# A TensorE planner that waits for room for two projections: half-array work, attention banks and the first loads of an attention and FFN kernel

## The chip, the cores and the metric

The kernel runs on one core of a Trainium2 chip. Times are device microseconds (us) of one execution. The kernel before takes 367.8 us (median of 3, 367.53 to 368.38). Most executions of one kernel agree within some 0.3%. A profile adds nothing visible: the profiled execution of before took 367.36 us by the same clock, of which 365.6 us lie between its first and last instruction ("span").

## The reference, cut to what matters

```python
# B=8 batches, H=8 heads, S=576 positions, D=64, 128 features; then an FFN over 4608 tokens
def phi(x):                                  # x: q or k
    proj = einsum('bhsd,df->bhsf', x, w_phi)
    proj = proj - max(abs(proj), axis=-1)
    return concatenate([exp(proj), exp(-proj)], axis=-1)
q_p, k_p = phi(q), phi(k)
kv  = einsum('bhsf,bhsd->bhfd', k_p, v);  z = sum(k_p, axis=2)
num = einsum('bhsf,bhfd->bhsd', q_p, kv)
den = einsum('bhsf,bhf->bhs', q_p, z)[..., None] + 1e-6
x   = (num / den) rearranged to [4608, 512]
out = square(relu(x @ w_in)) @ w_out         # w_in [512, 2048], w_out [2048, 512]
```

The heads have 64 channels, so the projections and the kv product use 64 of TensorE's 128 rows ("half-array" work, two row halves side by side). The product of q features with kv and the whole FFN use 128 rows ("full-array" work). By the ledger below, the FFN is 249 of 316 us of useful TensorE time.

## The kernel before

The kernel does not issue instructions in the order of its source. Every piece of work becomes an operation with a cost, a key (its place in a list of FFN units), its dependencies and its buffers. A planner then runs a small model of the engines and the loads, and the order that it finds is the program. In the trace of before, all 4,069 recorded matmuls of TensorE start in exactly this order, so a wrong guess of the planner becomes a wait on the chip. The part that chooses TensorE's next operation:

```python
SWITCH = 96
AHEAD, GROUP, LATE = 12, 2, 4

def pick(self, q, rows, can):
    now = min((it[0] for it in q if it[2].rows == 128), default=None)
    half = sorted(it for it in q if it[2].rows == 64 and can(it[2]))
    if now is None or now < 1 or not half:
        return None
    if rows == 64:                       # already in half-array work: stay
        go = half[0][0] < now + self.AHEAD
    else:                                # start it when one is late or two are overdue
        go = half[0][0] < now - self.LATE or (
            len([it for it in half if it[0] < now]) >= self.GROUP)
    # ... go: the first of half; otherwise the first full-array operation that can run
```

`can` asks whether the operation's buffers are free. All PSUM tiles come from one ring of eight banks; an attention operation takes a second token beside its bank, so that attention never holds more than `NATT` banks:

```python
NATT, LEAD, DUE, SPAN = 6, 3, 34, 28
r_one = ring("one", 8, [P, 512], F32, ps)      # eight PSUM banks
r_att = Ring(list(range(NATT)))                # tokens for attention
def banks(n):
    w = [Buf(r_one) for _ in range(n)]
    for x in w:
        x.token = Buf(r_att)
    return w
```

The first loads, all issued from GpSimd's queue, and what depends on them:

```python
FIRSTS = "k0 v0 q0 win k1 v1 wout q1"    # k0, v0, q0 in two halves, the rest whole
# ... ffn_in waits for all of w_in, ffn_out for all of w_out:
p_ = pe(key, 4 * (2 + TCH * 0.418), fn, xT_ops[c][a:z] + [o_win], [w, xT])
p_ = pe(key, 865, fn, [h2[c, mc, tt][2] for mc in mcs] + [o_wout], [w, out_] + ...)
```

In batches 0 and 1 ("fold") the maximum is not subtracted from k's projection; exp is taken from PSUM directly, and v is scaled by exp of the maximum instead, on GpSimd (line 523; in batch 1 five of the ten scalings run on VectorE). In the other batches VectorE subtracts the maximum (line 487, tile `ksh`), and v is only copied:

```python
if not fold:
    nc.vector.tensor_tensor(out=ksh.t[...], in0=wv(e), in1=mk.t[...], op=ALU.subtract)   # frees the PSUM bank
    # exp(+-) from ksh on ScalarE
else:
    # exp(+-) from PSUM on ScalarE, then for each of five groups and both signs:
    nc.gpsimd.tensor_tensor(out=y.t[...], in0=xv.t[...], in1=y.t[..., D]..., op=ALU.mult)
```

While TensorE has nothing to do in the start, the planner lets it multiply ones ("fillers"). Most operations of batch 0 come before the first FFN matmul; those of batches 1 to 7 are mixed with FFN work.

Of the kernel before, what the change touches and what calls it, by code (L numbers as in the profile page):

```python
# [45 lines left out]
class Plan:  # L46
# [30 lines left out]
    AHEAD, GROUP, LATE = 12, 2, 4  # L77

    def pick(self, q, rows, can):
# [4 lines left out]
        if rows == 64:  # L84
            go = half[0][0] < now + self.AHEAD
        else:
            go = half[0][0] < now - self.LATE or (
                len([it for it in half if it[0] < now]) >= self.GROUP)
# [97 lines left out]
def kernel(  # L186
# [10 lines left out]
    nc = tc.nc  # L197
# [51 lines left out]
    FOLD, VON = 2, ((1, 1), (0, 1))  # L249
    KTD = 1  # L250
    N0 = 43, 51
    NATT, LEAD, DUE, SPAN = 6, 3, 34, 28
# [6 lines left out]
    MARGIN = 200  # L259
    att = []  # L260

    def pe(key, cost, fn, deps=(), bufs=(), rows=128):
        o = pl.op("pe", cost, key, fn, deps, bufs, lat=350, rows=rows)
        att.append(o)
        return o

    def act(key, n, fn, deps=(), bufs=()):
        return pl.op("act", 60 + 0.83 * n, key, fn, deps, bufs, lat=220 + MARGIN)

    def dve(key, n, fn, deps=(), bufs=()):  # L270

        return pl.op("dve", 65 + 1.04 * n, key, fn, deps, bufs, lat=190 + MARGIN)

    def pool(key, cost, fn, deps=(), bufs=()):
        return pl.op("pool", cost, key, fn, deps, bufs, lat=150 + MARGIN)
# [56 lines left out]
    def load_x(b, name, key, dep=None, parts=1):  # L332

        t, r = src[name]
        buf = Buf(r)
        rows = t[b].rearrange("h s d -> (h s d)").rearrange("(pr t c) -> t pr c", pr=NPR, t=P)

        def fn(a, z):
# [4 lines left out]
        n = NPR // parts  # L343
        got[b, name] = buf, [[load(key + i / 10, 295 * n, 128 * n,
                                   lambda a=i * n: fn(a, a + n), [dep], [buf])]
                             for i in range(parts)]
# [4 lines left out]
    FIRSTS = "k0 v0 q0 win k1 v1 wout q1"  # L351
    for n, what in enumerate(FIRSTS.split()):
        if what == "win":
            o_win = load(FIRST + n, 4194, 512, lambda: nc.gpsimd.dma_start(out=win, in_=win_v))
        elif what == "wout":
            o_wout = load(FIRST + n, 4194, 2048,
                          lambda: nc.gpsimd.dma_start(out=wout, in_=wout_v))
        else:
            load_x(int(what[1]), what[0], FIRST + n, None, 2 if what[1] == "0" else 1)
# [29 lines left out]
    def attention(b, key):  # L389
# [5 lines left out]
        def transposes(xb, ld, xt, at):  # L395

            ops = []
            if b >= NPE[at]:
                for u0, n in GRP:
# [5 lines left out]
                    ops.append(xbar(key(at), n * 16, fn, ld[0] + (lq[0] if b > 1 else []), [xb, xt]))  # L405
                return ops
            for u0, n in ((0, 16), (16, 16), (32, 4)) if b or at else GRP:
                w, = banks(1)

                def fn(u0=u0, n=n, w=w):  # L410
                    for i in range(n // 2):
# [5 lines left out]
                        [o_id] + ld[0] + (ld[-1] if u0 + n > U // 2 else []), [w, xb, xt])  # L417
# [15 lines left out]

        tk = transposes(xk, lk, kT, 0)
# [8 lines left out]
        fold = b < FOLD  # L443
        va = [Buf(r_va), Buf(r_va)] if fold else [Buf(r_va)] * 2
        o_va = [[], []]
        if not fold:
            def fn():
                nc.gpsimd.memset(va[0].t[:, :, D], 1.0)
                nc.gpsimd.tensor_copy(out=va[0].t[:, :, :D], in_=xv.t)
            o_va = [[pool(key(32), 2400, fn, lv[0] + lv[-1], va[:1] + [xv])] * NG] * 2  # L450
# [4 lines left out]
        for g, (u0, n) in enumerate(GRP):  # L455
# [26 lines left out]
            if not fold:  # L482
# [10 lines left out]
                for t, sg in zip(ph, (1.0, -1.0)):  # L493
# [5 lines left out]
                    ke.append(act(kk, 2 * c, fn, d1, [t, ksh]))  # L499
# [13 lines left out]
            for s_, (y, sg) in enumerate(zip(va, (-1.0, 1.0))):  # L513
# [12 lines left out]
                deps = [o] + lv[0] + (lv[-1] if u0 + n > U // 2 else [])  # L526
# [12 lines left out]
        for hf in range(2):  # L539
# [6 lines left out]
            for prl in range(2):  # L546
                pr = 2 * hf + prl
                for s in range(2):
                    def fn(w=w, pr=pr, prl=prl, s=s):
                        for j in range(NJ):  # L550
# [3 lines left out]
                            for hi in range(2):  # L554
# [4 lines left out]
                                    rhs=va[s].t[r, u, : D + 1],  # L559
                                    start=(j == 0), stop=(j == NJ - 1))  # L560
                    gs = {(NJ * pr + j) // 8 for j in range(NJ)}
                    ops.append(pe(key(KV_AT[b > 0] + 8 * hf + 2 * (2 * prl + s)), 285, fn,
                                  [o_va[s][g] for g in gs] + [o for g in gs for o in (ke[2 * g + s] if fold else [ke[2 * g + s]])],
                                  w + [va[s]] + [kph[g][s] for g in gs], 64))
# [16 lines left out]
        for i, (g0, j0, nj) in enumerate(order_j):  # L581
# [144 lines left out]
            if hi_ == P and b == 0:  # L726
# [164 lines left out]
```

## Time and profile before

| | before |
|---|---|
| time, median | 367.8 us |
| span | 365.6 us |
| TensorE busy | 353.7 us (97%) |
| first FFN input matmul | 28.1 us |
| first FFN output matmul | 44.8 us |
| half-array runs on TensorE | 93 |

The page of the kernel before, cut: engines with busy time, share and instructions; then busy tenths in 40 slices of 9.1 us; then the chain of work that ended last.

```profile
span 365.6 us, 10343 instructions
...
PE 353.7 (97%) x4069; PEld 200.0 (55%) x4069; DVE 246.5 (67%) x553; ACT 242.3 (66%) x501; POOL 186.0 (51%) x289
...
PE   8899799999999999999999999999999999999994
...
POOL 8855745458837881787538764785445600000000
PEclk9999899999999999999999999999999999999999
DMA  7999962559755975488656944595520331121133
...
PE 82%; DVE 6%; DMA 3%; POOL 3%; SPq 2%; issue 2%; ACT 1%; DVEq 0%; POOLq 0%; ACTq 0%
```

TensorE is nearly always busy and owns 82% of the chain. The load engines are full from the second to the fifth slice (tenths of 9). But busy time is modelled from overlapping matmuls and hides what the engine loses, so the starts of matmuls have to be read. The timeline of TensorE alone (start us, duration us, engine, line, operation, output and inputs, rows x columns of the weights, size):

```profile
243.67 0.81 PE L762 MATMUL one<-xT,win 128*128 128x512 bf16 x3
244.31 0.29 PE L700 MATMUL one<-kv_sb,qph 128*128 128x65 bf16 x4
244.53 0.40 PE L632 MATMUL one<-wphi,qT 64*128 64x128 bf16 x8
244.86 0.39 PE L791 MATMUL one<-wout,h 128*128 128x512 bf16 x1
```

Read from start to start: four 65-column matmuls take 0.22 us here instead of the 4 x 31 ns that they take in a row, then eight half-array matmuls take 0.33 us before the next full-array one. Over the trace, from 60 us on, the medians are exact to some ns: a 512-column matmul is followed after 216 ns by another full-array matmul, and after 312 ns by a half-array one (48 cases). A 65-column matmul is followed after 31 ns by another, but after 125 to 128 ns by a half-array one. Back from half to full array the same 93 to 96 ns are lost. So each change of the array costs about 95 ns, and each half-array run two of them, 0.19 us.

That allows a ledger. *Useful* is each matmul at its steady start-to-start time as read from the trace (216 ns for 512 columns, 109 for 256, 56 for 128, 31 for 65; half-array pairs of 256 and 128 columns about 109 and 56; kv 16 each). *Changes* are array changes times 95 ns. *Fillers* are the ones-matmuls. *Gaps* are the rest between the first and the last matmul. Up to 47 matmul records of the output half are missing in some traces; they are counted as useful at 216 ns. A group of like matmuls that straddles 50 us is booked whole before it, so the useful work of a "0 to 50" column can be up to 0.9 us too high; cut strictly at 50 us it is 24.1 us before.

| ledger of before, us | 0 to 50 | from 50 | all |
|---|---|---|---|
| useful | 25.0 | 291.5 | 316.5 |
| changes | 3.4 | 14.2 | 17.7 (186) |
| fillers | 11.0 | 0 | 11.0 |
| gaps | 10.3 | 4.0 | 14.4 |

With 1.2 us before the first matmul and 4.8 us after the last one this adds up to the span. Useful work can't go away, so a gain must come from the start (25 us of use in 50 us), from changes or from gaps.

The waits of TensorE from 50 to 345 us name 1.8 of the 4.0 us of later gaps (engine, line, releaser: us, times, longest):

```profile
PE one L762 <- DVE ksh L487: 0.7, 1, 0.7
PE one L632 <- DMA qT<-xq: 0.6, 1, 0.6
PE one L600 <- DVE ksh L487: 0.3, 1, 0.3
PE one L791 <- DVE m L653: 0.2, 1, 0.2
```

In the start, GpSimd scales v. Its timeline from 9 to 24 us:

```profile
10.67 1.05 POOL L523 TENSOR_TENSOR va<-xv,va 128x512 bf16<-128x512 bf16 x1 [2.15 <-DMA xv<-in_v_dram]
11.68 1.22 POOL L357 DMA_DIRECT2D wout<-in_moe_w_out_dram  x1
12.91 3.09 POOL L523 TENSOR_TENSOR va<-xv,va 128x512 bf16<-128x512 bf16 x3
...
16.77 5.25 POOL L523 TENSOR_TENSOR va<-xv,va 128x512 bf16<-128x512 bf16 x6
```

The scalings end at 22.0 us, with w_out's issue among them; the first FFN matmul follows 6 us later. And in the page's fifth slice the granted clock falls (length, then busy us and count of each engine, granted clock, DMA share, GB/s):

```profile
core 0: us, PE busy (x) PEld busy (x) DVE busy (x) ACT busy (x) POOL busy (x), PEclk, DMA share, GB/s
40.00:43.40 3.40, 1.83 (x36) 1.55 (x33) 3.40 (x7) 3.40 (x10) 3.11 (x3) 1.00 1.22 209
43.40:46.80 3.40, 3.39 (x31) 1.68 (x28) 3.40 (x12) 2.49 (x7) 2.88 (x4) 0.50 1.21 207
```

For 3.4 us TensorE has half its clock (0.50), after 3.4 us in which it was busy for 1.83 us only.

### The profile page before, as it was taken

The page shows a single profiled execution, that of the slowest core. Times are in us where ns is not written, and L with a number is a line of the kernel's source. Part 1 is how long each engine was busy: PE and PEld are TensorE (multiplying, and loading weights), DVE is VectorE, ACT ScalarE, POOL GpSimd, SP SyncE. Part 2 cuts the span into 40 slices and gives each one's busy share as a digit, 9 for nine tenths or more (in the row PEclk, how much of TensorE's full clock was granted, in tenths as well). Part 3 has the DMA queues.
Part 4 walks back from the last instruction along what each step waited for, and adds up shares of the span by engine and source line. Part 5 has one row for each costly group of instructions (what it writes and reads, how often), then busy time and mean ns, then how long its engine had stood idle before and what let it go on. Part 6 is the DMA issues. An engine that isn't in the chain of part 4 may idle for free.

```text
span 365.6 us, 10343 instructions
## 1 busy us (share of the span) xinstructions
PE 353.7 (97%) x4069; PEld 200.0 (55%) x4069; DVE 246.5 (67%) x553; ACT 242.3 (66%) x501; POOL 186.0 (51%) x289
## 2 busy tenths in 40 slices
PE   8899799999999999999999999999999999999994
PEld 6679576766654555455545554454445544444442
DVE  2779969894789589868596868875886743332321
ACT  2997979689739983997479846985699633333300
POOL 8855745458837881787538764785445600000000
PEclk9999899999999999999999999999999999999999
DMA  7999962559755975488656944595520331121133
GB/s 110 208 209 208 208 119 59 90 85 166 133 102 81 173 147 103 87 161 157 94 102 113 176 96 100 90 216 87 109 64 22 74 82 34 29 48 41 29 72 73
DMA packets 68257, 39.81 MB, mean 109 GB/s; under 512 B 48624, under 2 KB 63088, under 8 KB 68208
## 3 DMA queue, kind: packets, MB, share of 16 engines
q0 software_dynamic: 15312, 18.35, 30.3%
q1 hardware_dynamic: 52896, 20.79, 28.7%
q8 instruction: 32, 0.52, 0.6%
q14 instruction: 17, 0.14, 0.1%
HBM read 36.77 MB, written 9.44 MB: 126 GB/s over the span
## 4 chain that ended last, share of the span: by engine, by line
PE 82%; DVE 6%; DMA 3%; POOL 3%; SPq 2%; issue 2%; ACT 1%; DVEq 0%; POOLq 0%; ACTq 0%
PE one L791 32%; PE one L762 31%; PE one L700 6%; PE one L556 4%; PE one L600 3%; PE one L632 3%; DVE mk L477 2%; POOL va L523 2%; DMA xv<-in_v_dram 2%; DVE ksh L487 2%; PE one L466 2%; SPq L401 2%; DMA qT<-xq 1%; PE one L366 1%; DVE ot L798 1%
## 5 line engine op out<-in xcount | busy, mean ns | idle before, releaser
L770 POOL TENSOR_TENSOR h<-hr 128x512 bf16<-128x512 bf16 x112 | 115.8, 1042 | 87.1 <-ACT hr L767 85.0
L762 PE MATMUL one<-xT,win 128*128 128x512 bf16 (+2 forms) x768 | 145.7, 326 | 0.9 <-DVE ksh L487 0.7
L791 PE MATMUL one<-wout,h 128*128 128x512 bf16 x576 | 145.9, 381 | 0.2 <-DVE m L653 0.2
L767 ACT ACTIVATE hr<-one 128x512 bf16<-128x512 f32 x144 | 85.3, 606 | 77.8 <-PE one L762 69.6
L762 PEld LDWEIGHTS <-win 128*128 128x128 bf16 x768 | 66.0, 98 | 50.4 <-issue 1.8
L791 PEld LDWEIGHTS <-h 128*128 128x128 bf16 x576 | 51.8, 98 | 57.3 <-issue 2.6
L607 ACT ACTIVATE qph<-one 128x512 bf16<-128x512 f32 (+1 forms) x160 | 78.0, 572 | 7.0 <-PE one L600 5.8
L495 ACT ACTIVATE kph<-ksh 128x1024 bf16<-128x1024 f32 (+1 forms) x60 | 54.9, 969 | 11.4 <-DVE ksh L487 10.9
L477 DVE TENSOR_REDUCE mk<-one 128x4 f32<-128x512 f32 (+1 forms) x80 | 49.3, 625 | 5.5 <-PE one L466 5.5
L653 DVE TENSOR_REDUCE m<-one 128x4 f32<-128x512 f32 (+1 forms) x60 | 35.5, 628 | 18.6 <-PE one L632 12.8
L798 DVE COPY ot<-one 128x512 f32<-128x512 f32 x36 | 24.7, 686 | 27.1 <-PE one L791 26.8
L710 DVE TENSOR_TENSOR one<-one,em 128x260 f32<-128x260 f32 (+1 forms) x80 | 32.0, 430 | 13.2 <-PE one L700 11.0
L487 DVE TENSOR_TENSOR ksh<-one,mk 128x512 f32<-128x512 f32 (+1 forms) x60 | 38.3, 638 | 3.3
L700 PEld LDWEIGHTS <-qph 128*128 128x128 bf16 x640 | 30.1, 98 | 16.4 <-issue 3.2
L700 PE MATMUL one<-kv_sb,qph 128*128 128x65 bf16 x640 | 34.7, 194 | 1.3 <-ACT kph L508 1.3
L721 DVE TENSOR_TENSOR xo<-one,rden 128x256 bf16<-128x256 f32 (+1 forms) x80 | 31.3, 417 | 0.6
L773 DVE TENSOR_TENSOR h<-hr 128x512 bf16<-128x512 bf16 x32 | 13.5, 422 | 23.3 <-ACT hr L767 23.3
L662 POOL COPY mq<-m 64x4 f32<-64x4 f32 x108 | 20.0, 185 | 9.4 <-DVE m L653 5.6
L556 PE MATMUL one<-va,kph 64*128 64x65 bf16 x1152 | 23.9, 191 | 0.2
L556 PEld LDWEIGHTS <-kph 64*128 64x128 bf16 x1152 | 21.2, 94 | 4.9 <-issue 4.4
L508 ACT ACTIVATE kph<-one 128x512 bf16<-128x512 f32 (+1 forms) x40 | 19.6, 605 | 2.1 <-DVE mk L477 2.1
L366 PE MATMUL one<-ones 128*128 128x256 bf16 x101 | 16.4, 305 | 1.2 <-DVE scrap L312 1.2
(46 smaller groups left out, 209.1 us busy)
## 6 DMA issues: line engine op xcount, KB each, us to landing
out_dram<-ot SPq DMA_DIRECT2D x72, 128.0 KB, 2.4
xk<-in_k_dram POOLq DMA_DIRECT2D x7, 576.0 KB, 6.4
xv<-in_v_dram POOLq DMA_DIRECT2D x7, 576.0 KB, 9.0
xq<-in_q_dram POOLq DMA_DIRECT2D x7, 576.0 KB, 11.8
win<-in_moe_w_in_dram POOLq DMA_DIRECT2D x1, 2048.0 KB, 18.8
wout<-in_moe_w_out_dram POOLq DMA_DIRECT2D x1, 2048.0 KB, 29.8
xk<-in_k_dram POOLq DMA_DIRECT2D x2, 288.0 KB, 5.3
xv<-in_v_dram POOLq DMA_DIRECT2D x2, 288.0 KB, 7.5
```

What stands on the lines that cost most here:

```text
L477: nc.vector.tensor_reduce(out=mk.t[:, e, ms], in_=wv(e), axis=AX.X, op=ALU.max, apply_absolute_value=True)
L487: nc.vector.tensor_tensor(out=ksh.t[:, e, : n // 2, :], in0=wv(e), in1=mk.t[:, e, ms].to_broadcast([P, n // 2, Fd]), op=ALU.subtract)
L495: nc.scalar.activation(out=t.t[:, :, : n // 2, :].rearrange("x e i f -> x e (i f)"), in_=ksh.t[:, :, : n // 2, :].rearrange("x e i f -> x ...
L556: nc.tensor.matmul(out=kvp(w, hi)[:, 2 * prl + s], lhsT=kph[g][s].t[r, i % 2, i // 2, :], rhs=va[s].t[r, u, : D + 1], start=(j == 0), stop ...
L607: nc.scalar.activation(out=t.t.rearrange("f (r b) hi p -> f b r hi p", b=2)[:, bk, :, :, lo:hi_], in_=w[bk].t[:, : nj * 256].rearrange("f ...
L653: d1 = [dve(kk, nj * 256, lambda w=w, m0=m0, nj=nj, bk=bk: nc.vector.tensor_reduce(out=m0.t[:, bk, : 2 * nj], in_=w[bk].t[:, : nj * 256].r ...
L700: nc.tensor.matmul(out=w.t[:, z * P : z * P + D + 1], lhsT=qg[s].t[:, h // 2, h % 2, :], rhs=kv[r][0].t[:, z % 2, z // 2, s, :], start=(s ...
L710: nc.vector.tensor_tensor(out=x, in0=x, in1=em.t[lo:hi_, hs].to_broadcast(list(x.shape)), op=ALU.mult)
L762: nc.tensor.matmul(out=w.t[:, y * n : (y + 1) * n], lhsT=win[:, kc, mc * P : (mc + 1) * P], rhs=xT.t[:, a:z, kc, :], start=(kc == 0), stop ...
L767: o = act(key - 4, TCH, lambda: nc.scalar.activation(out=r.t, in_=w.t, func=ACT.Relu), [p_], [w, r])
L770: o = pool(key - 4, 1050, lambda: nc.gpsimd.tensor_tensor(out=t.t, in0=r.t, in1=r.t, op=ALU.mult), [o], [r, t])
L791: nc.tensor.matmul(out=w.t, lhsT=h2[c, mc, tt][0].t[:, h2[c, mc, tt][1] :][:, :P], rhs=wout[:, mc, :], start=(mc == 0), stop=(mc == KC2 - 1))
```

## The change

Its intent, in its own words: TensorE's planner issues half-array work only when two projections fit into the free PSUM banks together, or when one is late; attention may hold seven banks; k0 is loaded in parts. The diff holds more than that: both weight matrices come in halves, each FFN group waits only for its half, and batches 0 and 1 scale v for three of the five groups; for the other two they subtract on VectorE like the later batches. The five scalings of batch 1 that VectorE made are moved or dropped with that. The planner's safety margins are cut in batch 0, batch 0's kv matmuls wait for fewer groups (`KVJ`), and the loads after the ninth get a later place in the plan.

```diff
-    AHEAD, GROUP, LATE = 12, 2, 4
+    AHEAD, GROUP, LATE = 24, 400, 8
+    EARLY = 3, 8
@@ pick, when TensorE is in full-array work
-            go = half[0][0] < now - self.LATE or (
-                len([it for it in half if it[0] < now]) >= self.GROUP)
+            go = half[0][0] < now - self.LATE
+            if not go and half[0][0] < now + self.EARLY[0]:
+                free, work = {}, 0
+                for it in half:
+                    if it[0] > now + self.EARLY[1]:
+                        break
+                    # ... need: how many buffers of each ring this operation still has to take
+                    if all(free.get(r, len(r.free)) >= n for r, n in need.items()):
+                        for r, n in need.items():
+                            free[r] = free.get(r, len(r.free)) - n
+                        work += it[2].cost
+                go = work >= self.GROUP
@@
-    FOLD, VON = 2, ((1, 1), (0, 1))
+    KVJ = 1
+    FG, VON = (3, 3), ((1, 1), (1, 1))       # groups of batches 0 and 1 that scale v
-    NATT, LEAD, DUE, SPAN = 6, 3, 34, 28
+    NATT, LEAD, DUE, SPAN = 7, 3, 34, 28
@@ margins of the planner
-    MARGIN = 200
+    MARGIN = 200
+    M0 = 40, 200, 350
+    slack = [M0[0]]                          # ... used for batch 0 in place of MARGIN
@@ first loads
-    FIRSTS = "k0 v0 q0 win k1 v1 wout q1"
+    FIRSTS = "k0:0-1 k0:1-2 k0:2-4 v0:0-2 v0:2-4 q0:0-2 q0:2-4 win:0-8 win:8-16 k1:0-4 v1:0-4 wout:0-8 q1:0-4 wout:8-16"
@@ ffn_in, ffn_out
-    ... xT_ops[c][a:z] + [o_win], [w, xT])
+    ... xT_ops[c][a:z] + [o_win[i * per + y] for y in range(per)], [w, xT])
-    ... for mc in mcs] + [o_wout],
+    ... for mc in mcs] + [o_wout[mc] for mc in mcs],
```

More of the change, by code (lines that the diff above doesn't have):

```diff
@@ L86, in pick @@
         else:
-            go = half[0][0] < now - self.LATE or (
-                len([it for it in half if it[0] < now]) >= self.GROUP)
+            go = half[0][0] < now - self.LATE
[4 more added lines that the diff above has]
+                        break
+                    new = {x for x in it[2].bufs if x.slot is None}
+                    need = {}
+                    for x in new:
+                        need[x.ring] = need.get(x.ring, 0) + 1
+                    if all(free.get(r, len(r.free)) >= n for r, n in need.items()):
[3 more added lines that the diff above has]
+                go = work >= self.GROUP
         if go:
@@ L247 @@
     r_ot = ring("ot", 2, [P, DM], F32)
-    FOLD, VON = 2, ((1, 1), (0, 1))
+    KVJ = 1
+    FG, VON = (3, 3), ((1, 1), (1, 1))
     KTD = 1
     N0 = 43, 51
-    NATT, LEAD, DUE, SPAN = 6, 3, 34, 28
+    PAIRS, XPE = 1, 1
+    NATT, LEAD, DUE, SPAN = 7, 3, 34, 28
     r_one = ring("one", 8, [P, 512], F32, ps)
@@ L259 @@
     MARGIN = 200
+    M0 = 40, 200, 350
+    slack = [M0[0]]
     att = []
     def pe(key, cost, fn, deps=(), bufs=(), rows=128):
-        o = pl.op("pe", cost, key, fn, deps, bufs, lat=350, rows=rows)
+        o = pl.op("pe", cost, key, fn, deps, bufs, lat=350 if slack[0] >= 100 else 240, rows=rows)
         att.append(o)
@@ L267, in act @@
     def act(key, n, fn, deps=(), bufs=()):
-        return pl.op("act", 60 + 0.83 * n, key, fn, deps, bufs, lat=220 + MARGIN)
+        return pl.op("act", 60 + 0.83 * n, key, fn, deps, bufs, lat=220 - 70 * (slack[0] < 100) + slack[0])
     def dve(key, n, fn, deps=(), bufs=()):
-        return pl.op("dve", 65 + 1.04 * n, key, fn, deps, bufs, lat=190 + MARGIN)
+        return pl.op("dve", 65 + 1.04 * n, key, fn, deps, bufs, lat=190 - 60 * (slack[0] < 100) + slack[0])
     def pool(key, cost, fn, deps=(), bufs=()):
-        return pl.op("pool", cost, key, fn, deps, bufs, lat=150 + MARGIN)
+        return pl.op("pool", cost, key, fn, deps, bufs, lat=150 + slack[0])
     queue, issues = [], []
@@ L330, with load_x, fn @@
     got = {}
-    def load_x(b, name, key, dep=None, parts=1):
+    def load_x(b, name, key, dep=None, a=0, z=NPR):
         t, r = src[name]
-        buf = Buf(r)
+        if (b, name) not in got:
+            got[b, name] = Buf(r), []
+        buf, parts = got[b, name]
         rows = t[b].rearrange("h s d -> (h s d)").rearrange("(pr t c) -> t pr c", pr=NPR, t=P)
-        def fn(a, z):
+        def fn():
             nc.gpsimd.dma_start(
@@ L342, in fn @@
             )
-        n = NPR // parts
-        got[b, name] = buf, [[load(key + i / 10, 295 * n, 128 * n,
-                                   lambda a=i * n: fn(a, a + n), [dep], [buf])]
-                             for i in range(parts)]
+        parts.append((a * NJ, load(key, 295 * (z - a), 128 * (z - a), fn, [dep], [buf])))
     win_v = moe_w_in.rearrange("(kc p) m -> p kc m", p=P)
@@ L350 @@
     o_id = pool(FIRST + 0.05, 700, lambda: make_identity(nc, ident))
-    FIRSTS = "k0 v0 q0 win k1 v1 wout q1"
+    FIRSTS = "k0:0-1 k0:1-2 k0:2-4 v0:0-2 v0:2-4 q0:0-2 q0:2-4 win:0-8 win:8-16 k1:0-4 v1:0-4 wout:0-8 q1:0-4 wout:8-16"
+    NEXT = 9
+    o_win, o_wout = {}, {}
     for n, what in enumerate(FIRSTS.split()):
+        what, a = what.split(":")
+        a, z = (int(x) for x in a.split("-"))
+        at = FIRST + n if n < NEXT else -160 + n
         if what == "win":
-            o_win = load(FIRST + n, 4194, 512, lambda: nc.gpsimd.dma_start(out=win, in_=win_v))
+            x = slice(a * P, z * P)
+            o = load(at, 262 * (z - a), 512, lambda x=x: nc.gpsimd.dma_start(
+                out=win[:, :, x], in_=win_v[:, :, x]))
+            o_win.update({mc: o for mc in range(a, z)})
         elif what == "wout":
-            o_wout = load(FIRST + n, 4194, 2048,
-                          lambda: nc.gpsimd.dma_start(out=wout, in_=wout_v))
+            o = load(at, 262 * (z - a), 128 * (z - a),
+                     lambda a=a, z=z: nc.gpsimd.dma_start(out=wout[:, a:z], in_=wout_v[:, a:z]))
+            o_wout.update({mc: o for mc in range(a, z)})
         else:
-            load_x(int(what[1]), what[0], FIRST + n, None, 2 if what[1] == "0" else 1)
+            load_x(int(what[1]), what[0], at, None, a, z)
     def loads(b, dep):
@@ L404, in fn @@
                         )
-                    ops.append(xbar(key(at), n * 16, fn, ld[0] + (lq[0] if b > 1 else []), [xb, xt]))
+                    ops.append(xbar(key(at), n * 16, fn, upto(ld, U) + (upto(lq, U) if b > 1 else []), [xb, xt]))
                 return ops
@@ L416, in transposes @@
                 p_ = pe(kk, 40 + n * 30, fn,
-                        [o_id] + ld[0] + (ld[-1] if u0 + n > U // 2 else []), [w, xb, xt])
+                        [o_id] + upto(ld, u0 + n), [w, xb, xt])
                 ms = slice(u0 // 2, (u0 + n) // 2)
@@ L432, in transposes @@
             return ops
+        slack[0] = M0[b] if b < 2 else MARGIN
         tk = transposes(xk, lk, kT, 0)
@@ L440, in attention @@
                 out=gate, in_=qT.t[:1, M - 1, P - 8 :]), [d], [qT])
-        fold = b < FOLD
-        va = [Buf(r_va), Buf(r_va)] if fold else [Buf(r_va)] * 2
+        slack[0] = M0[b] if b < 2 else MARGIN
+        nf = FG[b] if b < len(FG) else 0
+        va = [Buf(r_va), Buf(r_va)] if nf else [Buf(r_va)]
         o_va = [[], []]
-        if not fold:
+        if nf < NG:
+            us = slice(GRP[nf][0], U)
             def fn():
-                nc.gpsimd.memset(va[0].t[:, :, D], 1.0)
-                nc.gpsimd.tensor_copy(out=va[0].t[:, :, :D], in_=xv.t)
-            o_va = [[pool(key(32), 2400, fn, lv[0] + lv[-1], va[:1] + [xv])] * NG] * 2
+                nc.gpsimd.memset(va[0].t[:, us, D], 1.0)
+                nc.gpsimd.tensor_copy(out=va[0].t[:, us, :D], in_=xv.t[:, us])
+            o_plain = pool(key(32) if b else key(1), (U - us.start) * 66, fn, upto(lv, U), [va[0], xv])
         kph, ke = [], []
@@ L481, in attention @@
             d1 = []
-            if not fold:
+            if g >= nf:
                 ksh = Buf(r_ksh)
@@ L498, in fn @@
                             func=ACT.Exp, scale=sg)
-                    ke.append(act(kk, 2 * c, fn, d1, [t, ksh]))
+                    ke.append([act(kk, 2 * c, fn, d1, [t, ksh])])
+                for o in o_va:
+                    o.append(o_plain)
                 continue
@@ L525, in fn @@
                         in1=y.t[:, u0 : u0 + n, D].to_broadcast([P, n, D]), op=ALU.mult)
-                deps = [o] + lv[0] + (lv[-1] if u0 + n > U // 2 else [])
+                deps = [o] + upto(lv, u0 + n)
                 o_va[s_].append(pool(kk, n * 135, fn, deps, [y, xv]) if on else
@@ L558, in fn @@
                                     lhsT=kph[g][s].t[r, i % 2, i // 2, :],
-                                    rhs=va[s].t[r, u, : D + 1],
+                                    rhs=va[s if g < nf else 0].t[r, u, : D + 1],
                                     start=(j == 0), stop=(j == NJ - 1))
                     gs = {(NJ * pr + j) // 8 for j in range(NJ)}
+                    if b < KVJ:
+                        gs = {u // 8 for u in range(2 * NJ * hf, 2 * NJ * hf + 2 * NJ)}
                     ops.append(pe(key(KV_AT[b > 0] + 8 * hf + 2 * (2 * prl + s)), 285, fn,
-                                  [o_va[s][g] for g in gs] + [o for g in gs for o in (ke[2 * g + s] if fold else [ke[2 * g + s]])],
-                                  w + [va[s]] + [kph[g][s] for g in gs], 64))
+                                  [o_va[s][g] for g in gs] + [o for g in gs for o in ke[2 * g + s]],
+                                  w + va + [kph[g][s] for g in gs], 64))
             o = []
@@ L725, in attention @@
             nds.append(p_)
-            if hi_ == P and b == 0:
+            if hi_ == P and b < XPE:
                 w, = banks(1)
@@ L765, in fn @@
                         start=(kc == 0), stop=(kc == KC1 - 1))
-        p_ = pe(key, 4 * (2 + TCH * 0.418), fn, xT_ops[c][a:z] + [o_win], [w, xT])
+        p_ = pe(key, 4 * (2 + TCH * 0.418), fn, xT_ops[c][a:z] + [o_win[i * per + y] for y in range(per)], [w, xT])
         o = act(key - 4, TCH, lambda: nc.scalar.activation(
@@ L793, in fn @@
                     start=(mc == 0), stop=(mc == KC2 - 1))
-        p_ = pe(key, 865, fn, [h2[c, mc, tt][2] for mc in mcs] + [o_wout],
+        p_ = pe(key, 865, fn, [h2[c, mc, tt][2] for mc in mcs] + [o_wout[mc] for mc in mcs],
                 [w, out_] + [h2[c, mc, tt][0] for mc in mcs])
@@ L814 @@
         due[c] = n
-        if c == 1:
+        if 1 <= c <= PAIRS:
             ins = [(0, c, (i, a, a + 2)) for a in (0, 2) for i in range(8)]
@@ L830, with upto @@
             n += 1
+    def upto(ld, u):
+        return [o for a, o in ld if a < u]
     def place(b):
@@ L848 @@
     att.clear()
+    slack[0] = MARGIN
     for n, (what, c, i) in units:
```

## The prediction

> **What bounds the kernel now.** TensorE is busy 97% of the 365.6 us span, and the chain of waits is 82% TensorE. Busy time is modelled, so I read starts from the timeline: steady start-to-start is 216 ns for a 512-column matmul, 109 for 256, 31 for a 65-column one. Full-array FFN work begins at 28.1 us, its output half at 44.8 us. Adding these costs over the trace (my estimate): 316 us of useful matmul work, 18 us of changes between half-array (64-row) and full-array work, 11 us of fillers, 14 us of other gaps, 6 us before the first and after the last matmul. Only 25 us of useful work fits into the first 50 us; afterwards other gaps are about 4 us (largest 0.8 us). What can be won lies in the start and in the array changes.
>
> **Array changes.** After a 65-column matmul the next weight load starts 122 ns later for a half-array group, against 31; returning costs 148 ns against 53. That is 95 ns each way, 0.19 us per half-array run. The Trainium skill, "TensorE: Matmul & The Clock Gate", Part 2, says a weight load is pulled ahead when row groups don't conflict; at these borders it visibly isn't. By instruction order, before has 93 half-array runs and after 80; the 13 fewer all lie in the steady part (11 to about 9 per batch). Saving 13 x 0.19 = 2.5 us, all on the critical path.
>
> **Start.** Batch 0 is a latency chain: k0 lands (first transpose 6.4 us), v0 lands, ten GpSimd scalings of v run from 10.7 to 22.0 us with two DMA issues among them, kv finishes about 23 us, first FFN matmul 28.1 us. The change loads k0 in quarters (first transpose about 1 us earlier) and scales three of five groups: six scalings of 1.05 us plus a plain copy of about 0.9 us instead of eight of 1.05 and two of 0.66. That takes about 2.5 us from GpSimd and 2 us from ScalarE, and adds 2 us of subtraction to VectorE. For batch 1 VectorE also loses five scalings (6 us). First FFN matmul about 25 us, needing half of w_in (the whole lands about 25 us). w_out also comes in halves, so the first output matmuls don't need all 2 MB (now about 41.5 us). DMA is saturated until 50 us (208 GB/s); bytes are not saved. From 28 to 50 us there are 4.8 us of gaps, including a dip to half clock from 43.4 us for 3.4 us; half of them should go. Gain of the start: 4.5 us.
>
> **Seven attention banks, two-projection rule.** One more bank should remove about 1 of the 4 us of steady gaps; attention may now hold banks that FFN groups want. Net 0.5 to 1 us.
>
> **Sum.** 367.8 - 2.5 - 4.5 - 1 = about 359.8 us. Range 353.5 to 364.8. Chances: faster by over 2% 0.56, within 2% 0.41, slower 0.03.
>
> **What would show it.** First FFN matmul near 25 us, first output matmul near 40 us; 80 half-array runs at 95 ns a change; GpSimd scaling done by about 18.5 us; useful work before 50 us up from 25 to 30 us; afterwards no new waits over 1 us; tail unchanged.
>
> **What would make it wrong.** The start is limited by DMA (v0, w_in, w_out landing) rather than GpSimd and gains only 1 to 2 us; ScalarE, 87% busy from 28 to 50 us, takes over; bank starvation of the FFN; another clock dip; or, in my favour, steady gaps vanish entirely.

## The result, and the profile after

| | before | after |
|---|---|---|
| time, median | 367.9 us (4 runs, 367.53 to 368.38) | 359.23 us (4 runs, 358.90 to 359.46) |
| span | 365.6 us | 357.7 us |
| first FFN input matmul | 28.1 us | 26.8 us |
| first FFN output matmul | 44.8 us | 41.9 us |
| half-array runs | 93 | 80 |
| fillers | 101 | 83 |

The ratio is 0.9763, with a 95% interval of 0.9746 to 0.9780: faster by over 2%. A ratio here is the mean time of one kernel's fast runs over that of the other's of the same rounds, so it is not quite the ratio of the medians. Executions over 1.5% slower than the fastest of the same kernel are left out of the means.

| ledger, us | before | after | difference |
|---|---|---|---|
| useful, 0 to 50 us | 25.0 | 27.9 | +2.9 |
| fillers | 11.0 | 9.1 | -1.9 |
| changes | 17.7 (186) | 15.2 (160) | -2.5 |
| gaps, 0 to 50 us | 10.3 | 8.6 | -1.7 |
| gaps from 50 us | 4.0 | 2.3 | -1.7 |

Fillers, changes and gaps together fall by 7.8 us; the span falls by 7.9. (Cut strictly at 50 us, the first line is +3.3 us.) The page of the kernel after, the same lines:

```profile
span 357.7 us, 10261 instructions
...
PE 347.2 (97%) x4051; PEld 198.1 (55%) x4051; DVE 246.3 (69%) x556; ACT 240.4 (67%) x485; POOL 186.5 (52%) x293
...
PE   8799899999999999999999999999999999999994
...
POOL 8837964558827971689547754786436400000000
PEclk9999999999999999999999999999999999999999
DMA  7999992457945875479548755695441431121133
...
PE 88%; DVE 4%; ACT 3%; POOL 1%; issue 1%; ACTq 0%; DVEq 0%
```

The share of TensorE is the same 97%, which shows how little that number says: 8 us of losses have left a span in which nearly every tenth was 9 already. The waits of TensorE from 50 to 345 us:

```profile
PE one L734 <- issue: 0.3, 1, 0.3
PE one L796 <- DVE m L687: 0.2, 1, 0.2
```

The waits for `ksh` and `qT` are gone. GpSimd in the start (L555 is the scaling, L479 the plain copy, L382 the issue of w_out):

```profile
10.71 0.89 POOL L382 DMA_DIRECT2D wout<-in_moe_w_out_dram  x1 [1.11 <-DMA xv<-in_v_dram]
11.61 1.07 POOL L555 TENSOR_TENSOR va<-xv,va 128x512 bf16<-128x512 bf16 x1
...
12.65 0.83 POOL L479 COPY va<-xv 128x768 bf16<-128x768 bf16 x1
13.44 5.10 POOL L555 TENSOR_TENSOR va<-xv,va 128x512 bf16<-128x512 bf16 x5
...
19.30 0.89 POOL L382 DMA_DIRECT2D wout<-in_moe_w_out_dram  x1
```

The scalings end at 18.5 us instead of 22.0, yet the first FFN matmul comes only 1.3 us earlier. And the two halves of w_out are issued at 10.7 and 19.3 us. The half clock is gone too (window columns as before):

```profile
38.00:41.40 3.40, 2.01 (x42) 1.75 (x39) 2.93 (x8) 3.40 (x11) 3.40 (x5) 1.00 1.25 211
41.40:46.80 5.40, 5.10 (x103) 3.64 (x98) 5.22 (x11) 5.06 (x9) 5.02 (x5) 1.00 1.22 206
```

### The profile page after: what moved, and what is told of

It is laid out like the page before. It is cut to its first block, busy times and chain, and to the rows that moved or that the text cites. A ratio compares the mean times of both kernels' runs of the same rounds, so it can differ in the third digit from the quotient of the medians.

```text
span 357.7 us, 10261 instructions
## 1 busy us (share of the span) xinstructions
PE 347.2 (97%) x4051; PEld 198.1 (55%) x4051; DVE 246.3 (69%) x556; ACT 240.4 (67%) x485; POOL 186.5 (52%) x293
## 4 chain that ended last, share of the span: by engine, by line
PE 88%; DVE 4%; ACT 3%; POOL 1%; issue 1%; ACTq 0%; DVEq 0%
PE one L796 34%; PE one L825 34%; PE one L734 6%; PE one L588 4%; PE one L496 3%; PE one L634 2%; PE one L666 2%; ACT qph L641 2%; DVE mk L507 2%; PE one L392 2%; PE one L438 1%; DVE m L673 1%; ACT hr L801 1%; POOL va L479 1%; POOL h L804 1%
## 5 line engine op out<-in xcount | busy, mean ns | idle before, releaser
L825 PEld LDWEIGHTS <-h 128*128 128x128 bf16 x576 | 52.6, 98 | 58.5 <-issue 1.7
L641 ACT ACTIVATE qph<-one 128x512 bf16<-128x512 f32 (+1 forms) x160 | 77.0, 577 | 6.2 <-PE one L634 6.1
L525 ACT ACTIVATE kph<-ksh 128x1024 bf16<-128x1024 f32 (+1 forms) x68 | 61.2, 956 | 5.9 <-DVE ksh L517 5.8
L517 DVE TENSOR_TENSOR ksh<-one,mk 128x512 f32<-128x512 f32 (+1 forms) x68 | 42.8, 629 | 3.6
L734 PEld LDWEIGHTS <-qph 128*128 128x128 bf16 x640 | 29.1, 97 | 16.1 <-issue 3.3
L734 PE MATMUL one<-kv_sb,qph 128*128 128x65 bf16 x640 | 33.5, 194 | 1.8 <-DVE one L744 1.4
L588 PE MATMUL one<-va,kph 64*128 64x65 bf16 x1152 | 23.6, 190 | 0.9 <-POOL va L555 0.9
L751 DVE RECIPROCAL rden<-one 128x4 f32<-128x4 f32 (+1 forms) x80 | 12.6, 175 | 14.4 <-PE one L734 14.0
L666 PE MATMUL one<-wphi,qT 64*128 64x128 bf16 x296 | 15.5, 217 | 0.1
## 6 DMA issues: line engine op xcount, KB each, us to landing
win<-in_moe_w_in_dram POOLq DMA_DIRECT2D x2, 1024.0 KB, 15.6
```

What stands on the lines that cost most here:

```text
L517: nc.vector.tensor_tensor(out=ksh.t[:, e, : n // 2, :], in0=wv(e), in1=mk.t[:, e, ms].to_broadcast([P, n // 2, Fd]), op=ALU.subtract)
L525: nc.scalar.activation(out=t.t[:, :, : n // 2, :].rearrange("x e i f -> x e (i f)"), in_=ksh.t[:, :, : n // 2, :].rearrange("x e i f -> x ...
L588: nc.tensor.matmul(out=kvp(w, hi)[:, 2 * prl + s], lhsT=kph[g][s].t[r, i % 2, i // 2, :], rhs=va[s if g < nf else 0].t[r, u, : D + 1], sta ...
L641: nc.scalar.activation(out=t.t.rearrange("f (r b) hi p -> f b r hi p", b=2)[:, bk, :, :, lo:hi_], in_=w[bk].t[:, : nj * 256].rearrange("f ...
L734: nc.tensor.matmul(out=w.t[:, z * P : z * P + D + 1], lhsT=qg[s].t[:, h // 2, h % 2, :], rhs=kv[r][0].t[:, z % 2, z // 2, s, :], start=(s ...
L825: nc.tensor.matmul(out=w.t, lhsT=h2[c, mc, tt][0].t[:, h2[c, mc, tt][1] :][:, :P], rhs=wout[:, mc, :], start=(mc == 0), stop=(mc == KC2 - 1))
```

## The experiments

The question is which part of the change bought what. Twelve kernels ran. All gave correct results. One fact makes them hard to read: the planner is greedy, so any edit, also one in the start, reshuffles the order up to the end. The number of half-array runs of these kernels goes from 78 to 106. So each is read by its ledger, not by its time alone. How large the effect of a reshuffled order alone is shows in the last column: e13, e6 and e7 keep the rule and the banks of the changed kernel and edit only the start, and their gaps from 50 us on are 1.9, 2.1 and 5.3 us larger than its 2.3 us. Each row is one order, so a difference of that size in the late gaps is not safely the effect of the edit. ("By order" in the expectations means: counted in the built program, before it ran.)

| run | half-array runs | median us | ratio to before (95%) | useful 0-50 | changes | gaps 0-50 | gaps from 50 |
|---|---|---|---|---|---|---|---|
| before | 93 | 367.8 | | 25.0 | 17.7 | 10.3 | 4.0 |
| after | 80 | 359.23 | 0.9763 (0.9746-0.9780) | 27.9 | 15.2 | 8.6 | 2.3 |
| e1_old_rule | 93 | 369.11 | 1.0028 (1.0007-1.0048) | 27.9 | 17.7 | 8.3 | 7.7 |
| e2_six_banks | 86 | 359.25 | 0.9768 (0.9752-0.9783) | 28.8 | 16.4 | 7.6 | 2.3 |
| e10_old_rule_six | 101 | 363.89 | 0.9900 (0.9877-0.9923) | 28.8 | 19.2 | 7.6 | 3.5 |
| e3_rule_alone | 84 | 364.36 | 0.9906 (0.9889-0.9923) | 24.0 | 15.9 | 10.7 | 2.3 |
| e4_rule_and_banks | 91 | 368.05 | 1.0011 (0.9995-1.0027) | 23.4 | 17.3 | 10.9 | 4.4 |
| e12_before_w_halves | 106 | 370.57 | 1.0081 (1.0067-1.0094) | 27.9 | 20.1 | 7.1 | 7.3 |
| e7_w_whole | 89 | 370.06 | 1.0071 (1.0036-1.0105) | 24.3 | 16.9 | 11.9 | 7.6 |
| e13_win_whole | 87 | 362.70 | 0.9864 (0.9850-0.9877) | 27.5 | 16.5 | 8.7 | 4.2 |
| e5_scale_all_b0 | 85 | 363.82 | 0.9889 (0.9857-0.9920) | 28.4 | (slow profile) | 7.5 | (slow profile) |
| e6_k0_halves | 88 | 363.99 | 0.9906 (0.9878-0.9934) | 26.4 | 16.7 | 9.9 | 4.4 |
| c1_six_ahead32 | 82 | 359.05 | 0.9762 (0.9749-0.9775) | 27.9 | 15.6 | 8.1 | 1.9 |
| c2_seven_tuned | 78 | 358.24 | 0.9749 (0.9734-0.9764) | (slow profile) | | | |

The ledger is that of the one profiled execution, the time that of all. Where an e-run's profile differs from its median by a dip of the clock, the text says so.

### The rule and the banks: four kernels with the new start, three with the old

**e1_old_rule**: the changed kernel with the old rule.

```diff
-    AHEAD, GROUP, LATE = 24, 400, 8
-    EARLY = 3, 8
+    AHEAD, GROUP, LATE = 12, 2, 4
# and the old lines of pick
```

> The changed kernel with the old rule for half-array work (start it when two are overdue), all else kept: by order 93 half-array runs instead of 80. Border theory (each half-array run costs 0.19 us in two changes, nothing else): 13 x 0.19 = +2.5 us, so about 361.7 us, other gaps unchanged. Rival (the rule pays because it waits for free banks, the borders are incidental): other gaps after 50 us rise from 2.4 us by 1.5 us or more, so 363 us or more.

Measured: 369.11 us, slower than the kernel before. The start is untouched (27.9 us of use in 50 us). The ledger has 2.5 us more of changes, as the border theory says, but also 5.4 us more of gaps from 50 us on. Both theories hold a part; the rival's is the larger. The waits of TensorE from 50 to 345 us of this run (L782 is the FFN input matmul, L503 the subtraction that frees a bank of k's projection):

```profile
PE one L782 <- DVE ksh L503: 2.5, 4, 0.7
PE one L574 <- issue: 1.5, 1, 1.5
```

and its timeline at the first of the four cases:

```profile
112.68 0.81 PE L782 MATMUL one<-xT,win 128*128 128x512 bf16 x3
113.42 0.28 PE L482 MATMUL one<-wphi,kT 64*128 64x128 bf16 x4
114.42 1.02 PE L782 MATMUL one<-xT,win 128*128 128x512 bf16 x4 [0.72 <-DVE ksh L503]
```

After half-array work for k, TensorE stands at an FFN input group that needs a bank, and each bank that could serve is still held by a projection which VectorE has not subtracted. TensorE works in order, so nothing else fills the 0.72 us. This is what the new rule prevents: it starts half-array work when there is room for it, so less is squeezed in. Another 1.5 us is a stop within a kv group at 197.6 us for which the profile names no cause ("issue"); such stops of 0.6 to 1.7 us stand in some other runs too, and their cause is open. The profiled execution was also the fastest of its six (367.01 us, clock 0.998); the others took 368.6 to 369.5 us at a clock of 0.995, see the last section. Of the 5.4 us of gaps the 1.5 us stop has no shown cause and speaks for neither theory.

**e2_six_banks**: the changed kernel with one bank fewer.

```diff
-    NATT, LEAD, DUE, SPAN = 7, 3, 34, 28
+    NATT, LEAD, DUE, SPAN = 6, 3, 34, 28
```

> The changed kernel with six attention banks instead of seven: by order 86 half-array runs instead of 80. Border theory: +6 x 0.19 = +1.1 us, about 360.4 us. Bank theory (the seventh bank itself removes waits): the gaps after 50 us also rise, by about 1.5 us, so 361.5 us or more.

Measured: 359.25 us, the same as with seven. The bank theory falls: the gaps from 50 us on are the same 2.3 us. The border theory misses too, in total: its 1.1 us of changes are there, and the start, which this edit should not touch, returned them (first FFN matmul at 25.1 us instead of 26.8, 0.9 us more use before 50 us).

**e10_old_rule_six**: the old rule and six banks with the new start (both edits above).

> The changed kernel with the old rule and six banks (its start kept): by order 101 half-array runs, 21 more than the changed kernel. Borders alone: +4.0 us, 363.2 us. If the old rule also makes waits for banks (as it did with seven banks, 5.4 us of them): gaps after 50 us 4 us or more instead of 2.3, total 365 to 369 us. If those waits needed the seventh bank: gaps stay near 2.3 us.

Measured: 363.89 us, and gaps of 3.5 us from 50 us on. The border theory's 363.2 us is missed by 0.7 us, and the gaps lie between the two expectations (2.3 and 4 us): most of the waits that made e1 slow did need the seventh bank, not all. TensorE's waits for `ksh` in this run:

```profile
PE one L782 <- DVE ksh L503: 0.7, 1, 0.7
PE one L620 <- DVE ksh L503: 0.4, 1, 0.4
```

1.1 us instead of 2.5. (Against e2, which has the same start: 2.8 us of changes and 1.2 us of gaps from 50 us on make 4.0 of the 4.1 us between the spans, 361.7 and 357.6.)

**e3_rule_alone**: the kernel before with only the new rule.

```diff
-    AHEAD, GROUP, LATE = 12, 2, 4
+    AHEAD, GROUP, LATE = 24, 400, 8
+    EARLY = 3, 8
# and the new lines of pick
```

> The kernel before with nothing but the new rule: by order 84 half-array runs instead of 93. Border theory: -9 x 0.19 = -1.7 us, about 366.2 us, start (first FFN matmul at 28.1 us) unchanged. Rival (the rule needs the seventh bank): no gain, about 367.9 us, with new gaps of 1.7 us in the steady part.

Measured: 364.36 us, a gain of 3.5 us, twice what the border theory gives, and the rival (no gain without the seventh bank) falls. The changes fell by 1.8 us and the gaps from 50 us on by 1.7 us, to the same 2.3 us as in the changed kernel. The start, expected to stay, did not quite: the first FFN matmul came at 28.3 us, but the first output matmul at 48.3 instead of 44.8 us, with 24.0 us of use before 50 us instead of 25.0.

**e4_rule_and_banks**: e3 with seven banks.

> The kernel before with the new rule and seven attention banks: by order 91 half-array runs. Border theory: -2 x 0.19 = -0.4 us, about 367.5 us, worse than the rule alone. Bank theory: the seventh bank removes about 2 us of steady gaps whatever the count of runs, so 366 us or less.

Measured: 368.05 us, no gain left. The seventh bank costs 3.7 us here: 1.4 us of changes, 2.1 us of gaps from 50 us on (among them one unexplained stop of 1.7 us in a kv group), the rest in the start. Its largest wait is in the start, and it's another than e1's, so why seven banks hurt this kernel is not settled by one cause.

Together, as differences of medians:

| | new rule instead of old | seven banks instead of six |
|---|---|---|
| new start, six banks | 363.89 to 359.25: -4.6 us | |
| new start, seven banks | 369.11 to 359.23: -9.9 us | |
| old start, six banks | 367.83 to 364.36: -3.5 us | |
| new start, new rule | | 359.25 to 359.23: 0.0 us |
| new start, old rule | | 363.89 to 369.11: +5.2 us |
| old start, new rule | | 364.36 to 368.05: +3.7 us |

The rule is worth 3.5 to 4.6 us at six banks, a half to two thirds of it array changes (1.8 of 3.5 and 2.8 of 4.1 us by the ledgers), most of the rest gaps. In the two entries with e1 (9.9 and 5.2 us) about 2 us are the distance of its median from its profiled run; that dips of the clock explain it is not shown (last section). The rule gained in all three pairs; its size carries the scatter of the order named above. The seventh bank never gained anything.

### The start: which load, which engine

**e7_w_whole**: both weight matrices in one piece.

```diff
-    ... win:0-8 win:8-16 k1:0-4 v1:0-4 wout:0-8 q1:0-4 wout:8-16
+    ... win:0-16 k1:0-4 v1:0-4 wout:0-16 q1:0-4
-    NEXT = 9
+    NEXT = 8
```

> The changed kernel with each FFN weight matrix loaded in one piece again. If the halves matter: the first FFN matmul or the first output matmul waits for a weight load (the profile names it) and comes 1 us or more later than 26.8 and 41.9 us. If not: both within 0.5 us, total changed only by the borders (89 half-array runs by order, +1.7 us).

Measured: 370.06 us. The first output matmul comes at 51.2 us instead of 41.9, and useful work before 50 us falls from 27.9 to 24.3 us: all that the start had gained, and more. But TensorE waited for no weights: this is the tile view of w_out in this run (operation and duration, first and last start; then us from issue to landing):

```profile
L825 PE MATMUL one<-wout,h x533: 376/379/391, 51.2 to 363.2; 128*128 128x512 bf16 x178
L382 POOL DMA_DIRECT2D wout<-in_moe_w_out_dram x1: 1220/1220/1220, 17.5 to 17.5; - x1
...
DMA to landing us min/median/max: 23.6/23.6/23.6
```

and the same view of the kernel before and of the kernel after:

```profile
L791 PE MATMUL one<-wout,h x576: 376/379/634, 44.8 to 360.5; 128*128 128x512 bf16 x192
L357 POOL DMA_DIRECT2D wout<-in_moe_w_out_dram x1: 1220/1220/1220, 11.7 to 11.7; - x1
...
DMA to landing us min/median/max: 29.8/29.8/29.8
```

```profile
L825 PE MATMUL one<-wout,h x576: 376/379/390, 41.9 to 352.6; 128*128 128x512 bf16 x192
L382 POOL DMA_DIRECT2D wout<-in_moe_w_out_dram x2: 889/890/892, 10.7 to 19.3; - x2
...
DMA to landing us min/median/max: 24.6/24.9/25.3
```

In e7 the 2 MB were issued at 17.5 us and landed 23.6 us later, at about 41 us; the first output matmul started 10 us after that, without a wait. So it stood late in the order. The planner puts a matmul into the order only after its own model has let the load land, which is how a whole w_out delays the output half. The runs show only that neither the landing nor a wait on the chip did it; but the planner is part of each kernel.py and runs without the chip (the first FFN matmul, planned for 26.9 us in the changed kernel, came at 26.8). In its model w_out lands at 47.5 us in the kernel before and at 48.1 us in e7, its first half at 41.8 us in the changed kernel and in e13, and the first output matmul is planned for 47.5, 49.7, 42.3 and 42.2 us, never more than 1.6 us after the modelled landing. On the chip w_out landed at about 41.5 us in the kernel before and 41.1 us in e7, and the first half, issued at 10.7 us in the changed kernel, at about 36 us: the model is 6 to 7 us late. So the whole w_out of the kernel before had landed by the time, 41.9 us, at which the changed kernel starts its output half, and what the halves remove is a delay that the planner imposes on itself. Whether correcting the model of the loads would gain the same with whole matrices was not tested. Of the 10.6 us between the spans of e7 and the changed kernel, 5.3 us are gaps from 50 us on.

**e13_win_whole**: w_in whole, w_out in halves.

> The changed kernel with w_in in one piece, w_out still in halves; by order 87 half-array runs (+1.3 us for borders). If only w_out's halves mattered in the run with both whole: first output matmul near 42 us, useful work before 50 us 27 us or more, total about 360.5 us. If w_in's halves carry it: first FFN matmul 28 us or later, useful work before 50 us near 24.3 us, total 364 us or more.

Measured: first output matmul at 41.6 us, 27.5 us of use before 50 us. So w_out's halves carry it (e7 differs from this run by w_out alone: 51.2 us and 24.3 us). First FFN matmul at 28.1 instead of 26.8 us: w_in's halves bring the first input groups forward, which is made up for by 50 us. The total of 362.70 us is 2.2 us above what the first theory asks; 1.9 us of that are gaps from 50 us on, put down to the reshuffled order.

**e12_before_w_halves**: the kernel before with only this, and the old start otherwise.

```diff
-    FIRSTS = "k0 v0 q0 win k1 v1 wout q1"
+    FIRSTS = "k0 v0 q0 winA winB k1 v1 woutA q1 woutB"
# each FFN group depends on its half
```

> The kernel before with nothing but each weight matrix loaded in two halves. By order 106 half-array runs instead of 93: borders alone +2.5 us. If the halves are what the start gained from: first output matmul at 42 us or earlier instead of 44.8, useful work before 50 us from 25.0 to 27 us or more, total about 368 us. If they only help together with the lighter start: first output matmul and work before 50 us unchanged within 0.7 us, total about 370 us.

Measured: first output matmul at 41.8 us, 27.9 us of use before 50 us: as much as in the changed kernel, without its quarters of k0, its subtractions and its margins (the first FFN matmul stays at 28.0 us). The total is worse than before (370.57 us), because the old rule makes 106 half-array runs of the new order and 7.3 us of gaps from 50 us on. A real gain in the start was given back later.

**e5_scale_all_b0**: batch 0 scales all five groups on GpSimd again.

```diff
-    FG, VON = (3, 3), ((1, 1), (1, 1))
+    FG, VON = (5, 3), ((1, 1), (1, 1))
```

> The changed kernel, but batch 0 scales v for all five groups again (batch 1 still three): ten scalings on GpSimd, no subtraction on VectorE in batch 0. GpSimd theory (the prediction's: the scalings are the chain of the start): scaling ends 2.5 us later than 18.5 us, first FFN matmul 2 us or more later than 26.8 us, useful work before 50 us down from 27.9 to about 26. VectorE theory (the subtractions that replaced them took the chain over, so the trade was nearly even): scaling ends later but the first FFN matmul moves less than 1 us and useful work before 50 us stays within 0.7 us. Half-array runs by order 85 (+0.95 us for the borders in either case).

The profile of this run fell in the slow state (368.03 us; TensorE stood for 3.55 us from 84.3 us on, behind VectorE, which waited 3.42 us for a store, and had half its clock for 6.8 us from 87 us on), so only the first 50 us are read, where nothing was disturbed, and with that reserve. The scalings ended at 21.0 us, 2.5 us later. The first FFN matmul came 1.1 us later, between the two theories; useful work before 50 us was 28.4 us, not less than the 27.9 us of the changed kernel. So by 50 us the GpSimd theory has fallen; of the 2.5 us of later scaling, 1.1 us reached the first FFN matmul. That VectorE took the chain over is not shown by this either: by then it is the output half that counts. The fast runs (362.58 to 364.02 us) are some 4 us slower than the changed kernel; 0.95 us of that are five more half-array runs, the rest is not broken down.

**e6_k0_halves**: k0 in halves.

> The changed kernel with k0 loaded in two halves as before instead of quarter, quarter, half. If the early quarter starts the chain: first transpose about 6.4 instead of 5.9 us, and the first FFN matmul later by the same 0.5 to 1 us. If v0 or VectorE sets the pace: first transpose later, first FFN matmul unchanged within 0.3 us. Half-array runs by order 88, so the borders alone ask for +1.5 us in the total.

Measured: first FFN matmul at 27.9 us, 1.1 us later, and 26.4 us of use before 50 us. The waits of TensorE in this run begin with the load:

```profile
PE one L438 <- DMA xk<-in_k_dram: 2.2, 1, 2.2
```

But the first transpose, expected at 6.4 instead of 5.9 us, came at 5.70 us (5.87 in the changed kernel): the quarter did not start the chain earlier. What came later is the second piece of k0: its transposes began at 9.8 us, those of the changed kernel's later pieces at 7.4 to 9.5 us. In the kernel before, which loads the same halves, that wait was 0.3 us, so its 2.2 us are not the halves alone. How much of the 1.1 us, and of the 1.5 us of use, is the edit's own stays open: in this execution TensorE also had half its clock for 3.4 us from 11.0 us on.

### Two tries to beat both

With six banks and the rule reaching further ahead (c1), or with seven and some other planner constants (c2):

```diff
# c1
-    AHEAD, GROUP, LATE = 24, 400, 8
+    AHEAD, GROUP, LATE = 32, 400, 8
-    NATT, LEAD, DUE, SPAN = 7, 3, 34, 28
+    NATT, LEAD, DUE, SPAN = 6, 3, 34, 28
# c2
+    AHEAD, GROUP, LATE = 32, 400, 6
+    NATT, LEAD, DUE, SPAN = 7, 3, 33, 30
+    KTD = 2
```

> A try to beat both: the changed kernel with six attention banks and half-array runs that may reach 32 units ahead instead of 24; by order 82 half-array runs. From the six-bank run's ledger (28.8 us of useful work before 50 us, 2.3 us of gaps after, 86 runs) and four runs fewer: 359.2 - 4 x 0.19 = about 358.5 us. If looking further ahead brings back waits for banks: 360 us or more.

> Another try: seven banks, half-array runs up to 32 units ahead, late after 6, attention placed one unit later over 30 units, the second k0 copy on ScalarE; by order 78 half-array runs. Borders alone: -0.4 us against the changed kernel, about 358.8 us. If the copy on ScalarE frees VectorE in the start (the VectorE theory of the start): first FFN matmul 25.5 us or earlier instead of 26.8 and about 357.5 us.

c1 took 359.05 us: the expected 358.5 us was not reached, as the start lost the 0.9 us of use that e2 had. c1's interval, too, overlaps that of the changed kernel: no proven gain. c2 took 358.24 us (median of all five; its four fast runs took 357.94 to 359.32), the fastest of all, but its interval (0.9734 to 0.9764) overlaps that of the changed kernel (0.9746 to 0.9780), so it's no proven gain. Its profile fell into an odd execution (last section), so whether the copy on ScalarE helped its start is not known.

## Why the prediction was right or wrong

The total was right: 359.8 us predicted, 359.23 measured, and "faster by over 2%" was the likelier class at 0.56. Its parts:

1. *Array changes, 2.5 us.* Right. 13 half-array runs fewer, 95 ns for each change in both traces (312 ns instead of 216 after a 512-column matmul), 186 changes to 160: 2.5 us. The rule did more, though: it also removed most of the 1.7 us of gaps from 50 us on (e3, with the old start, shows the same 2.3 us of gaps left). One number of the prediction is read loosely: 31 ns is the distance of two 65-column matmuls; the next weight load starts 2 ns after the matmul before it there, and 122 ns after it at a border, so it is pulled ahead in the one place and not in the other, as the prediction says.
2. *Start, 4.5 us.* Too large, and for the wrong reason. Useful work before 50 us rose by 2.9 us (3.3 cut strictly), not by 5; the first FFN matmul came at 26.8 us, not 25, the first output matmul at 41.9 us, not 40. The step that failed is "Batch 0 is a latency chain ... ten GpSimd scalings": GpSimd did end at 18.5 us, as predicted to the tenth, and that bought little (putting it back costs the first FFN matmul 1.1 us in e5, and no useful work by 50 us). e12 reaches the same 27.9 us with all ten scalings in place, e5 with them put back. What bought the start is w_out in halves, which the prediction mentioned in one clause, and not by the load's landing, as it said there, but by the planner's order (e7).
3. *Half of the 4.8 us of gaps between 28 and 50 us should go.* Right in size: over 30 to 50 us the gaps went from 4.8 to 2.3 us. Near 1 us of it is the half clock from 43.4 us: its four 512-column matmuls started 426 ns apart instead of 216 (0.8 us). This dip goes with the whole w_out: the profiles of before, e3, e4 and e7 have one from 43.4 to 46.2 us on, none of the nine profiles with w_out in halves that hold a clock record has one between 15 and 80 us. That the late output half causes it was not tested.
4. *The seventh bank should remove about 1 us.* Wrong: 0.0 us with the new rule (e2), and a loss of 3.7 and 5.2 us in the other two pairs. The gaps from 50 us on did fall, by 1.7 us, but the rule did that.
5. *No new wait over 1 us, tail unchanged.* Right: the largest gap from 50 us on is 0.44 us, and 4.8 us follow the last matmul in both.

So the number was right partly by luck: an overestimate of the start (4.5 for about 3 us) met an underestimate of the rule.

## What to carry to other kernels

When TensorE is 97% busy, write a ledger of start-to-start times, array changes, fillers and gaps: it shows what a busy share hides, and where in the kernel a part of a change acts, though not apart from the reshuffling that any edit brings to a scheduled kernel. Where a planner makes the order, compare its modelled landing times with the trace's: here it let w_out land 6 to 7 us too late. Count the borders between half-array and full-array work and start half-array work only when its output banks are free, since in an in-order engine a group that finds no bank stops everything. Split a late large load by what its first reader needs, and test each part of a bundled change alone and taken away: here one part (the seventh bank) was worth nothing, and one (weights in halves) made the kernel slower when it stood alone.

## What the Trainium skill lacked or had wrong

- The Trainium skill, "TensorEngine Tiling (Array Packing)", Tiling Modes, says that changing the tiling mode drains TensorE, but gives no cost. Here a change between 64-row and 128-row work costs about 95 ns each way: 312 instead of 216 ns after a 512-column matmul (48 cases in before, 39 in after).
- The Trainium skill, "TensorE: Matmul & The Clock Gate", Part 2 (Back-to-back issue gap), gives a sustained spacing of about 131 ns for 512 columns and about 81 ns for 128 in real kernels. These traces show 216 and 56 ns in long rows, the figures that this section keeps for an isolated matmul.
- The same page, Part 1, has the half clock set in after an idle window of about 3.4 us. The length agrees: the half clocks within the traces of before, e3, e4, e5, e6 and e7 last 3.41 us (6.83 in e5), and each begins a whole number of 3.41 us (2 to 24) after its clock record does. TensorE stood before two of them, 3.55 us in e5 and 2.2 us in e6. It wasn't idle ahead of the others: in before it was busy for 1.83 us of the 3.4 us ahead, in 36 matmuls, in e7 for 2.26 us. What sets the half clock off is not shown here, as windows with 2.12 us (e12, 40.1 to 43.6 us) and 1.95 us (e1, 196.6 to 200.0 us) brought none. What one costs isn't settled: e1's run at clock 0.998 took 367.01 us, its five at 0.995 took 368.55 to 369.47; e6's two at 0.995 took 364.32 and 364.90, its others 363.30 and 363.66; but the kernel before has a median of 368.0 us in 14 runs at 0.995 or less and 367.5 us in 13 at 0.996 or more.
- The same page warns that clock records can't be fully trusted. Here one is missing: an execution of c2 took 1223.25 us instead of 358, and its trace holds no clock record at all (the 1.0 in its result only says that no loss was recorded). TensorE alone was slow: its 512-column matmuls start 840 ns apart in the median, not 216. Why is not shown. Cut from its page (group, count, busy us, mean ns of one, idle):

```profile
span 1221.4 us, 10218 instructions
...
L796 PE MATMUL one<-xT,win 128*128 128x512 bf16 (+2 forms) x768 | 500.6, 889 | 0.5 <-issue 0.5
...
L801 ACT ACTIVATE hr<-one 128x512 bf16<-128x512 f32 x144 | 86.0, 599 | 671.1 <-PE one L796 619.4
```

The FFN input matmul has a mean of 889 ns instead of 326, while ScalarE's activation has 599 ns against 608 in the changed kernel.
- No page that was read names the stops of 0.6 to 1.7 us inside a group of kv matmuls without a recorded wait (e1 at 197.6 us, e4 at 167.3 us, e6 at 166.9 us). Their cause is open.
